# Converting float64 weights on three engines instead of one, in a fused attention and MLP kernel

## The chip, the cores and the metric

The kernel runs on one core of a Trainium2 chip. The metric is the time of one execution on the device in microseconds (us); six executions of the kernel before gave a median of 894.68 us (893.46 to 895.31).

The core has five engines with a queue of instructions each. TensorE (PE in the profile) multiplies matrices and transposes; a matrix multiply in float32 leaves two records in the profile. VectorE (DVE), ScalarE (ACT) and GpSimd (POOL) work on elements. SyncE (SP) only issues data transfers (DMAs) here. An engine works through its queue strictly in order: an instruction that waits for a semaphore holds up all that stands behind it, also where that would have been ready.

## The reference

`x` is 8 batches x 8 heads x 512 positions x 64, `state` is 8 x 8 x 32 x 64, both float32. Attention goes both ways, and its result, 544 rows of 512 for each batch, passes through an MLP:

```
scores  = scale * x @ state.T;     a  = softmax(scores);   xread = a  @ state     # 512 rows of each batch
scores2 = scale * state @ x.T;     a2 = softmax(scores2);  sread = a2 @ x         # 32 rows of each batch
y   = concat([xread, sread]) as (8*544, 512)
h   = y @ w_in                                 # 512 -> 2048
g   = h * erf(softplus(h))
out = g @ w_out                                # 2048 -> 512
```

The weights come as float64: they are made by multiplying a float32 array with a float64 scalar. Each of the two matrices is 8.4 MB. [...] `hi` holds the sign, 11 bits of exponent and the top 20 bits of the fraction, `lo` the other 32 bits.

## The kernel before, in words

**Tiles and stages.** Rows of 128 partitions are used throughout. The hidden width of 2048 is cut into four groups g of 512 (`GF` = 4 blocks of 128 each). The main loop goes over nine chunks: chunk b = 0 to 7 is the 512 x-rows of batch b, chunk 8 is the 256 state rows of all batches. For each chunk and group:

- `mixed(b, g)` (lines 224 to 235) multiplies the batch's states with group g of w_in. As xread is a @ state, the hidden layer of the x-rows is a @ (state @ w_in), which needs a contraction over 256 (8 heads x 32 states) instead of 512. The two halves of the result are copied out of PSUM by ScalarE (line 233) and VectorE (line 234).
- `hidden` (237 to 252) makes h for four blocks: matmuls (246), Softplus on ScalarE (248), a copy of h on VectorE into the tile `hs` (249), then one Erf over all four blocks (250) and one product with `hs` (251). Softplus, Erf and Exp need different tables, and each change of table is an instruction of its own on ScalarE.
- `project` (254 to 260) multiplies the result with group g of w_out (257) and accumulates in PSUM over the groups. It is held back as `pending` and issued after the next group's `hidden`.
- `store` copies the sums out and writes them to memory.

`attention(b)` (139 to 220) transposes x (145), makes the scores (155), copies them to `sc` (159), transposes them back (170), and takes a softmax over the 32 states for the x half (173, 174, 180, 184 to 187); these probabilities are transposed to `aT` (199, 201), an operand of `hidden`. The states' half takes the other softmax, over 512 positions (178, 179, 181), transposes it (193, 195), multiplies with x (212), scales (217), transposes (219) and leaves the result in `sT` (220), which only chunk 8 reads. Attention 0 stands ahead of the main loop; attention b + 1 is issued in group 1 of chunk b.

**Weights.** In chunk 0 each group starts with `weights_in(g)`, `mixed(0, g)` and `weights_out(g)`. Each of the two loads two tiles, so there are 16 weight tiles of 128 x 1024 numbers, 1 MB as float64. `weight` (81 to 110) loads one into the tile `hs`, a pool tag with two buffers that `hidden` uses too, and converts it with seven instructions on VectorE: exponent out of `hi` (96), rebased (98), clamped and put into place (99), sign merged (100), fraction out of `hi` (103), `lo` added (106), fraction times exponent (108).

**Order.** A scheduler places every instruction in its engine's queue when the kernel is built, from the order and dependencies of the program; at run time the queues are fixed. DMAs of SP are in such a queue too. At the start SP issues eight x loads of batch 0 (67), eight state loads (75), two w_in tiles (90), and the x loads of batch 1. A completion semaphore can be shared by several DMAs, and a DMA that uses one again waits for the DMA before.

Of the kernel before, what the change touches and what calls it, by code (L numbers as in the profile page):

```python
# [16 lines left out]
def kernel(  # L17
# [54 lines left out]
    st = const.tile([P, B, P], F32, name="st")  # L72
    for h in range(H):
        i, e = h // 2, h % 2
        nc.sync.dma_start(out=st[Ns * i:Ns * i + Ns, :, D * e:D * e + D],
                          in_=state[:, h].rearrange("b n d -> n b d"))

    w_in = const.tile([P, NK, d_ff], F32, name="w_in")
    w_out = const.tile([P, NF, d_model], F32, name="w_out")

    def weight(dst, src, shape):


        if src.dtype == F32:
            nc.sync.dma_start(out=dst, in_=src)
            return
        i = shape[1]
        n = shape[0] * i
        raw = act.tile([P, 2 * n], U32, name="hs")
        nc.sync.dma_start(out=raw.rearrange("p (o i) -> p o i", i=2 * i), in_=src.bitcast(U32))  # L90
        words = raw.rearrange("p (n w) -> p n w", w=2)
        lo, hi = words[:, :, 0], words[:, :, 1]

        em = act.tile([P, 2, n], U32, name="s", bufs=3)
        e, m = em[:, 0], em[:, 1]
        nc.vector.tensor_scalar(e, hi, 20, 0x7FF, op0=ALU.logical_shift_right,  # L96
                                op1=ALU.bitwise_and)
        nc.vector.tensor_scalar(e, e, -896.0, 0.0, op0=ALU.add, op1=ALU.max)  # L98
        nc.vector.tensor_scalar(e, e, 255.0, 8388608.0, op0=ALU.min, op1=ALU.mult)
        nc.vector.scalar_tensor_tensor(out=e, in0=hi, scalar=0x80000000, in1=e,  # L100
                                       op0=ALU.bitwise_and, op1=ALU.bitwise_or)

        nc.vector.tensor_scalar(m, hi, 0xFFFFF, 0x100000, op0=ALU.bitwise_and,  # L103
                                op1=ALU.bitwise_or)
        f = m.bitcast(F32)
        nc.vector.scalar_tensor_tensor(out=f, in0=lo, scalar=2.0 ** -32, in1=m,  # L106
                                       op0=ALU.mult, op1=ALU.add)
        nc.vector.scalar_tensor_tensor(  # L108
            out=dst, in0=f.rearrange("p (o i) -> p o i", i=i), scalar=2.0 ** -20,
            in1=e.bitcast(F32).rearrange("p (o i) -> p o i", i=i), op0=ALU.mult, op1=ALU.mult)  # L110

    gw = GF * P

    def weights_in(g):
        fs = slice(gw * g, gw * g + gw)
        for k in range(0, NK, 2):
            weight(w_in[:, k:k + 2, fs],
                   moe_w_in[P * k:P * k + 2 * P, fs].rearrange("(k p) f -> p k f", p=P),
                   (2, gw))

    def weights_out(g):
        for t in range(GF * g, GF * g + GF, 2):
            weight(w_out[:, t:t + 2, :],
                   moe_w_out[P * t:P * t + 2 * P].rearrange("(t p) e -> p t e", p=P),
                   (2, d_model))


    sT = const.tile([P, NK, B, Ns], F32, name="sT")
# [8 lines left out]
        nc.scalar.copy(stT[b], ps)  # L137

    def attention(b):
        xt = x_t.pop(b)  # L140
        xT = att.tile([P, NI, S], F32, name="xT")
        for i in range(NI):
            xp = ps_at.tile([P, S], F32, name="at")
            for c in range(NC):
                nc.tensor.transpose(out=xp[:, P * c:P * c + P], in_=xt[:, c, 2 * i:2 * i + 2, :],  # L145
                                    identity=ident)
            nc.scalar.copy(xT[:, i, :], xp)  # L147

        s2 = [ps_at.tile([P, S], F32, name="at") for _ in range(2)]
        for i in range(NI):
            for e in range(2):
                r, q = slice(D * e, D * e + D), slice(Ns * i, Ns * i + Ns)
                nc.tensor.matmul(out=s2[e][q, :], lhsT=stT[b][r, q], rhs=xT[r, i, :],  # L155
                                 start=True, stop=True)
        sc = att.tile([P, 2, S], F32, name="sc")
        for e in range(2):
            nc.scalar.copy(sc[:, e], s2[e])

        a = att.tile([P, 2, NC * NI, Ns], F32, name="a")
        a2 = att.tile([P, 2, S], F32, name="a2")
        a2T = att.tile([P, 2, NC, P], F32, name="a2T")
        aT[b] = keep.tile([P, 2, S], F32, name="aT")
        z2 = small.tile([P, 2], F32, name="z2")
        for e in range(2):

            s1 = ps_at.tile([P, NC * NI, Ns], F32, name="at")
            for c in range(NC):
                nc.tensor.transpose(out=s1[:, NI * c:NI * c + NI, :],  # L170
                                    in_=sc[:, e, P * c:P * c + P], identity=ident)
            m1 = small.tile([P, NC * NI], F32, name="m1")
            nc.vector.reduce_max(out=m1, in_=s1, axis=AX.X)
            nc.vector.tensor_tensor(a[:, e], s1, m1.unsqueeze(2).to_broadcast([P, NC * NI, Ns]),
                                    op=ALU.subtract)

            m2 = small.tile([P, 1], F32, name="m2")
            nc.vector.reduce_max(out=m2, in_=sc[:, e], axis=AX.X)
            nc.vector.tensor_scalar(m2, m2, -scale, None, op0=ALU.mult)
            nc.scalar.activation(out=a[:, e], in_=a[:, e], func=ACTF.Exp, scale=scale)  # L180
            nc.scalar.activation(out=a2[:, e], in_=sc[:, e], func=ACTF.Exp, bias=m2, scale=scale,
                                 accum_out=z2[:, e:e + 1])
            z1 = small.tile([P, NC * NI], F32, name="z1")
            nc.vector.reduce_sum(out=z1, in_=a[:, e], axis=AX.X)
            nc.vector.tensor_scalar(z1, z1, 1e-9, None, op0=ALU.add)
            nc.vector.reciprocal(z1, z1)
            nc.vector.tensor_tensor(a[:, e], a[:, e],
                                    z1.unsqueeze(2).to_broadcast([P, NC * NI, Ns]), op=ALU.mult)

        for e in range(2):  # L190
            ps = ps_at.tile([P, NC, P], F32, name="at")
            for c in range(NC):
                nc.tensor.transpose(out=ps[:, c, :], in_=a2[:, e, P * c:P * c + P],  # L193
                                    identity=ident)
            nc.scalar.copy(a2T[:, e], ps)
        for e in range(2):
            ps = ps_at.tile([P, S], F32, name="at")
            for c in range(NC):
                nc.tensor.transpose(out=ps[:, P * c:P * c + P],  # L199
                                    in_=a[:, e, NI * c:NI * c + NI, :], identity=ident)  # L200
            nc.vector.tensor_copy(aT[b][:, e], ps)

        nc.vector.tensor_scalar(z2, z2, 1e-9, None, op0=ALU.add)
        nc.vector.reciprocal(z2, z2)
        sr = ps_at.tile([P, 2, D], F32, name="at")
        for e in range(2):
            for c in range(NC):
                for i in range(NI):  # L210
                    q = slice(Ns * i, Ns * i + Ns)
                    nc.tensor.matmul(out=sr[q, e, :], lhsT=a2T[:, e, c, q],  # L212
                                     rhs=xt[:, c, 2 * i + e, :],
                                     start=(c == 0), stop=(c == NC - 1))
        sn = small.tile([P, 2, D], F32, name="sn")
        for e in range(2):
            nc.vector.tensor_scalar(sn[:, e], sr[:, e], z2[:, e:e + 1], None, op0=ALU.mult)
        ps = ps_at.tile([P, NI, Ns], F32, name="at")
        nc.tensor.transpose(out=ps, in_=sn, identity=ident)
        nc.scalar.copy(sT[:, :, b, :], ps)  # L220

    m_t = {}

# [62 lines left out]
                for k in range(NK)]  # L286

    states(0)
    attention(0)
    chunks = [(S, put_x(b)) for b in range(B)] + [(B * Ns, put_s)]  # L290
    pending = None
    for b, (n, put) in enumerate(chunks):
        acc = None
        for g in range(NG):
            if b == 0:
                weights_in(g)
                mixed(0, g)
                weights_out(g)
            if b + 1 < B and g == 0:
                load_x(b + 1)  # L300
                states(b + 1)
            gT = hidden(pairs(b, g), n)
            if pending is not None:
                pending()
            if acc is None:
                acc = [ps_o.tile([P, d_model], F32, name="o%d" % r) for r in range(n // P)]

            def pending(gT=gT, n=n, g=g, acc=acc, put=put):
                project(gT, n, g, acc)
                if g == NG - 1:  # L310
                    store(acc, n, put)
            if b + 1 < B:
                mixed(b + 1, g)
                if g == 1:
                    attention(b + 1)
    pending()


# [28 lines left out]
```

## Time and profile before

| what | value |
|---|---|
| median of six executions | 894.68 us |
| the profiled execution | 893.46 us, of it 891.7 us between the first and the last instruction (span) |
| mean granted TensorE clock | 0.976 of full speed |
| busy time of TensorE | 836.6 us (94%) |
| busy time of VectorE | 355.2 us (40%) |
| busy time of ScalarE | 351.8 us (39%) |
| busy time of GpSimd | 0.7 us |
| median from issue to landing, 1 MB w_in tile | 5.2 us |
| median from issue to landing, 128 KB x load | 3.0 us |

The shares of busy time are means over two very different stretches, the loading and converting of weights at the start and the rest, and so have to be read by windows. A line of a table of groups names the source line, the engine, the operation, the written and read tiles, the shape and the count; then the busy time in us and the mean of one in ns, then the idle time in front of them and what ended it. A line of the chain of waits has a start, a length and what took it: the chain is followed back from the last instruction to what released it.

### The profile page before, as it was taken

Reading aid. Unit: us, or ns where it says so; the run is one execution under the profiler, and the core shown is the slowest. Engines: PE = TensorE matmul, PEld = TensorE weight load, DVE = VectorE, ACT = ScalarE, POOL = GpSimd, SP = SyncE. Lnnn points to the kernel's source line nnn. Section 1 sums busy time; section 2 is a strip of 40 time slices with the busy share of each in tenths; the row PEclk is TensorE's granted clock in tenths of the full one; section 3 lists DMA queues with packets and bytes.
Section 4 is the critical chain, followed back from the end, with each engine's and each line's share of the span. In section 5 each row is a group of like instructions: output and inputs, shape, how many; then the busy total and the mean of one; then the engine's idle time right before and its main releaser. Section 6 shows DMA issues by size and latency. Waiting matters only on the chain.

```text
span 891.7 us, 7809 instructions
## 1 busy us (share of the span) xinstructions
PE 836.6 (94%) x3216; PEld 379.2 (43%) x3216; DVE 355.2 (40%) x500; ACT 351.8 (39%) x460; POOL 0.7 (0%) x6
## 2 busy tenths in 40 slices
PE   3659868999999999999999999999999999999997
PEld 1313423344444444445444544444444444445664
DVE  3888988523422252226222522234222522222121
ACT  2221530544434453437333633444344534333342
POOL 0000000000000000000000000000000000000000
PEclk9579988999999999999999999999999999999999
DMA  8432254010201020101000020100010000000100
GB/s 212 142 133 103 95 142 142 0 48 0 49 0 48 0 49 0 39 10 36 13 24 24 1 48 0 48 0 1 0 48 0 1 1 35 12 0 1 47 1 24
DMA packets 45346, 35.09 MB, mean 39 GB/s; under 512 B 36864, under 2 KB 36864, under 8 KB 45312
## 3 DMA queue, kind: packets, MB, share of 16 engines
q1 hardware_dynamic: 45312, 34.61, 12.7%
q8 instruction: 25, 0.41, 0.2%
q14 instruction: 9, 0.07, 0.0%
HBM read 25.69 MB, written 8.91 MB: 39 GB/s over the span
## 4 chain that ended last, share of the span: by engine, by line
PE 83%; DVE 11%; DMA 3%; SPq 1%; ACT 1%; issue 0%; DVEq 0%
PE o L257 49%; PE h L246 26%; PE at L231 3%; DMA hs<-in_moe_w_in_dram 2%; DVE s L106 2%; DVE s L100 2%; PE at L145 1%; DVE s L251 1%; DVE s L96 1%; PE at L212 1%; DVE s L103 1%; DVE s L98 1%; DMA hs<-in_moe_w_out_dram 1%; PE at L155 1%; PE at L199 1%; PE at L193 1%
## 5 line engine op out<-in xcount | busy, mean ns | idle before, releaser
L257 PE MATMUL o<-w_out,s 128*128 128x512 f32 x1088 | 488.6, 597 | 14.9 <-DVE s L251 14.9
L257 PEld LDWEIGHTS o<-w_out,s 128*128 128x128 f32 x1088 | 204.1, 191 | 260.4 <-issue 241.1
L246 PE MATMUL h<-aT,m 128*128 128x512 f32 x512 | 242.2, 609 | 6.5 <-DVE hs L249 6.5
L249 DVE COPY hs<-h 128x512 f32<-128x512 f32 (+1 forms) x144 | 95.1, 661 | 247.1 <-ACT s L248 247.1
L248 ACT ACTIVATE s<-h 128x512 f32<-128x512 f32 (+1 forms) x144 | 82.3, 574 | 186.9 <-PE h L246 186.5
L246 PEld LDWEIGHTS h<-aT,m 128*128 128x128 f32 x512 | 94.5, 193 | 132.1 <-issue 117.8
L251 DVE TENSOR_TENSOR s<-s,hs 128x2048 f32<-128x2048 f32 (+1 forms) x36 | 78.2, 2173 | 74.7 <-ACT s L250 74.7
L233 ACT COPY m<-at 128x512 f32<-128x512 f32 x32 | 18.7, 586 | 210.8 <-PE at L231 210.8
L234 DVE COPY m<-at 128x512 f32<-128x512 f32 x32 | 22.1, 691 | 166.4 <-PE at L231 166.4
L250 ACT ACTIVATE s<-s 128x2048 f32<-128x2048 f32 (+1 forms) x36 | 65.3, 1815 | 0.4
L248 ACT ACT_TABLE_LOAD x42 | 53.9, 1283 | 14.2 <-DVE w_out L108 13.5
L231 PE MATMUL at<-w_in,stT 64*32 64x512 f32 x512 | 42.4, 622 | 6.0 <-DVE w_in L108 5.6
L250 ACT ACT_TABLE_LOAD x36 | 46.2, 1283 | 0.6
L265 ACT COPY ot<-o 128x512 f32<-128x512 f32 x34 | 19.8, 582 | 65.1 <-PE o L257 65.1
L246 PE MATMUL h<-sT,w_in 128*128 128x256 f32 x128 | 28.9, 379 | 0.0
L246 PEld LDWEIGHTS h<-sT,w_in 128*128 128x128 f32 x128 | 24.3, 190 | 6.7 <-issue 3.8
L231 PEld LDWEIGHTS at<-w_in,stT 64*32 64x32 f32 x512 | 6.7, 106 | 35.4 <-issue 22.6
L145 PE MATMUL at<-ident,x 128*128 128x128 f32 x128 | 18.4, 293 | 2.3 <-DVE m L234 2.1
L145 PEld LDWEIGHTS at<-ident,x 128*128 128x128 f32 x128 | 16.1, 151 | 10.2 <-ACT m L233 3.0
L96 DVE TENSOR_SCALAR s<-hs 128x1024 uint32<-128x1024 uint32 x16 | 11.0, 690 | 23.4 <-DMA hs<-in_moe_w_in_dram 22.4
L147 ACT COPY xT<-at 128x512 f32<-128x512 f32 x32 | 17.4, 590 | 7.1 <-PE at L145 7.1
L106 DVE SCALAR_TENSOR_TENSOR s<-hs,s 128x1024 f32<-128x1024 uint32 x16 | 19.5, 1221 | 0.1
(47 smaller groups left out, 296.2 us busy)
## 6 DMA issues: line engine op xcount, KB each, us to landing
x<-in_x_dram SPq DMA_DIRECT2D x64, 128.0 KB, 3.0
hs<-in_moe_w_in_dram SPq DMA_DIRECT2D x8, 1024.0 KB, 5.2
hs<-in_moe_w_out_dram SPq DMA_DIRECT2D x8, 1024.0 KB, 5.5
out_dram<-ot SPq DMA_DIRECT2D x32, 256.0 KB, 2.3
st<-in_state_dram SPq DMA_DIRECT2D x8, 64.0 KB, 2.1
out_dram<-ot SPq DMA_DIRECT2D x8, 64.0 KB, 1.7
```

The costliest lines, as they stand in the source:

```text
L96: nc.vector.tensor_scalar(e, hi, 20, 0x7FF, op0=ALU.logical_shift_right, op1=ALU.bitwise_and)
L106: nc.vector.scalar_tensor_tensor(out=f, in0=lo, scalar=2.0 ** -32, in1=m, op0=ALU.mult, op1=ALU.add)
L145: nc.tensor.transpose(out=xp[:, P * c:P * c + P], in_=xt[:, c, 2 * i:2 * i + 2, :], identity=ident)
L231: nc.tensor.matmul(out=ps[e][q, :], lhsT=stT[b][r, q], rhs=w_in[r, i, gw * g:gw * g + gw], start=True, stop=True)
L234: nc.vector.tensor_copy(mg[:, 1], ps[1])
L246: nc.tensor.matmul(out=hp[:, 0:n], lhsT=lhsT[:, P * i:P * i + P], rhs=rhs, start=(k == 0), stop=(k == len(pairs) - 1))
L248: nc.scalar.activation(out=s[:, i, :], in_=hp[:, 0:n], func=ACTF.Softplus)
L249: nc.vector.tensor_copy(hs[:, i, :], hp[:, 0:n])
L250: nc.scalar.activation(out=s, in_=s, func=ACTF.Erf)
L251: nc.vector.tensor_tensor(s, s, hs, op=ALU.mult)
L257: nc.tensor.matmul(out=acc[r], lhsT=gT[:, i, P * r:P * r + P], rhs=w_out[:, GF * g + i, :], start=(g == 0 and i == 0), stop=(g == NG - 1 a ...
L265: nc.scalar.copy(ot, acc[r])
```

## The change

Four things change.

1. The conversion. `hi`, read as a float32 number, has the float64's exponent in the wrong place by three bits. It is multiplied by 2^-112 (GpSimd), which rebases the exponent; the bits are shifted left by 3 (VectorE), which makes room for the lower bits and drops the old sign; `lo` is scaled by 2^-29 into an integer of up to 3 bits (ScalarE); both are added as integers (GpSimd); and the sign bit of `hi` is merged in (VectorE). The steps work in place in the destination, the scaling in place in the raw tile.
2. The raw tiles of w_in have a tag `raw` with two buffers of their own; those of w_out stay with `hs`. The tag `s` isn't used by the conversion any more.
3. The eight state loads are issued from ScalarE's queue.
4. The states' half of `attention` becomes an inner function `rest`. For batch 0 it is called after `hidden` of chunk 0, group 0; for the others right after `attention`.

```
-        nc.sync.dma_start(out=st[Ns * i:Ns * i + Ns, :, D * e:D * e + D],
-                          in_=state[:, h].rearrange("b n d -> n b d"))
+        nc.scalar.dma_start(out=st[Ns * i:Ns * i + Ns, :, D * e:D * e + D],
+                            in_=state[:, h].rearrange("b n d -> n b d"))
...
-    def weight(dst, src, shape):
+    def weight(dst, src, shape, tag, bufs):
...
-        n = shape[0] * i
-        raw = act.tile([P, 2 * n], U32, name="hs")
-        nc.sync.dma_start(out=raw.rearrange("p (o i) -> p o i", i=2 * i), in_=src.bitcast(U32))
-        words = raw.rearrange("p (n w) -> p n w", w=2)
-        lo, hi = words[:, :, 0], words[:, :, 1]
-
-        em = act.tile([P, 2, n], U32, name="s", bufs=3)
-        e, m = em[:, 0], em[:, 1]
-        nc.vector.tensor_scalar(e, hi, 20, 0x7FF, op0=ALU.logical_shift_right,
-                                op1=ALU.bitwise_and)
-        nc.vector.tensor_scalar(e, e, -896.0, 0.0, op0=ALU.add, op1=ALU.max)
-        nc.vector.tensor_scalar(e, e, 255.0, 8388608.0, op0=ALU.min, op1=ALU.mult)
-        nc.vector.scalar_tensor_tensor(out=e, in0=hi, scalar=0x80000000, in1=e,
+        raw = act.tile([P, 2 * shape[0] * i], U32, name=tag, bufs=bufs)
+        raw = raw.rearrange("p (o i) -> p o i", i=2 * i)
+        nc.sync.dma_start(out=raw, in_=src.bitcast(U32))
+        words = raw.rearrange("p o (i w) -> p o i w", w=2)
+        lo, hi = words[:, :, :, 0], words[:, :, :, 1]
+        d = dst.bitcast(U32)
+        nc.gpsimd.tensor_scalar(dst, hi.bitcast(F32), 2.0 ** -112, None, op0=ALU.mult)
+        nc.scalar.activation(out=lo, in_=lo, func=ACTF.Copy, scale=2.0 ** -29)
+        nc.vector.tensor_scalar(d, d, 3, None, op0=ALU.logical_shift_left)
+        nc.gpsimd.tensor_tensor(d, d, lo, op=ALU.add)
+        nc.vector.scalar_tensor_tensor(out=d, in0=hi, scalar=0x80000000, in1=d,
                                        op0=ALU.bitwise_and, op1=ALU.bitwise_or)
-
-        nc.vector.tensor_scalar(m, hi, 0xFFFFF, 0x100000, op0=ALU.bitwise_and,
-                                op1=ALU.bitwise_or)
-        f = m.bitcast(F32)
-        nc.vector.scalar_tensor_tensor(out=f, in0=lo, scalar=2.0 ** -32, in1=m,
-                                       op0=ALU.mult, op1=ALU.add)
-        nc.vector.scalar_tensor_tensor(
-            out=dst, in0=f.rearrange("p (o i) -> p o i", i=i), scalar=2.0 ** -20,
-            in1=e.bitcast(F32).rearrange("p (o i) -> p o i", i=i), op0=ALU.mult, op1=ALU.mult)
...
-                   (2, gw))
+                   (2, gw), "raw", 2)
...
-                   (2, d_model))
+                   (2, d_model), "hs", 2)
...
+        def rest():
+            a2 = att.tile([P, 2, S], F32, name="a2")
...
+        return rest
...
-    attention(0)
+    rest = attention(0)
...
             gT = hidden(pairs(b, g), n)
+            if b == 0 and g == 0:
+                rest()
             if pending is not None:
                 pending()
...
-                    attention(b + 1)
+                    attention(b + 1)()
```

The queues of the changed kernel, as its build fixes them, differ from those of before at these places. On VectorE the first reduction of attention 0 stands behind the shift of w_out's second tile; the copy of mixed(0,0) behind the merge of the third w_in tile; the product of chunk 0, group 0 behind the shift of the third w_out tile. On ScalarE the copy of the first states behind the scaling of the first w_in tile, and the copies of the scores behind the scaling of the second w_out tile. On TensorE hidden(0,1) stands behind the first matmul of group 0's projection, where before it stood ahead of all of it. On SP all four weight loads of group 0 stand ahead of the x loads of batch 1, and the last two w_out loads behind the x loads of batch 3.

## The prediction

> **What bounds the kernel now.** I read the page's totals first, then busy time by stretches of 20 us, then the groups of the first 165 us, then the chain and the order of time there. The stretches split the run in two (per stretch: length, busy PE, PEld, DVE, ACT, POOL, then the granted clock, the DMA share and GB/s):
>
> ```profile
> 20.00:40.00 20.00, 10.48 (x98) 5.01 (x97) 17.74 (x34) 4.52 (x10) 0.00 (x0) 0.58 0.56 151
> 60.00:80.00 20.00, 16.07 (x43) 5.70 (x44) 17.22 (x20) 0.94 (x2) 0.00 (x0) 0.83 0.44 158
> 120.00:140.00 20.00, 10.16 (x32) 3.33 (x27) 16.08 (x19) 6.81 (x8) 0.00 (x0) 0.74 0.30 96
> ...
> 0.00:165.00 165.00, 115.82 (x532) 48.44 (x532) 131.27 (x181) 45.70 (x67) 0.70 (x6) 0.88 0.43 131
> 165.00:891.70 726.70, 720.77 (x2690) 330.79 (x2684) 223.88 (x319) 306.12 (x393) 0.00 (x0) 1.00 0.06 19
> ```
>
> From 165 us on TensorE is busy without gaps at full clock, and the change touches nothing there. Before it VectorE (DVE) is the full engine, and TensorE has holes in which its clock drops to a half. The conversions fill VectorE (busy us, mean ns of one):
>
> ```profile
> L106 DVE SCALAR_TENSOR_TENSOR s<-hs,s 128x1024 f32<-128x1024 uint32 x16 | 19.5, 1221 | 0.1
> L100 DVE SCALAR_TENSOR_TENSOR s<-hs,s 128x1024 uint32<-128x1024 uint32 x16 | 19.5, 1220 | 0.0
> L98 DVE TENSOR_SCALAR s<-s 128x1024 uint32<-128x1024 uint32 x16 | 11.0, 686 | 0.0
> ```
>
> Back to back they start 0.60 us (one input) and 1.13 us (two inputs) apart, as the chain of waits shows, with the product that ends group 0 and the rate of TensorE once it runs (start, us, what):
>
> ```profile
> 58.08 1.13 DVE s L106
> 59.22 1.13 DVE s L100
> 60.35 2.21 DVE s L251
> ...
> 70.10 0.69 DVE s L96
> ...
> 123.57 0.61 DVE hs L249
> ...
> 154.33 5.15 PE o L257 x12
> ```
>
> So the measure for the change is TensorE's lost time: time passed less its work at full clock, 0.43 us per 512-wide record (5.15/12). By 165 us TensorE did 96 projection and 64 hidden records (160 x 0.43 = 68.8), 8 mixed (1.1 each, 8.8) and two attentions (7.4 each, 14.8): 92.4, so 72.6 us are lost. Only that can shrink.
>
> **Part by part.** *VectorE.* A tile's seven instructions (4 x 0.60 + 3 x 1.13 = 5.8 us, 93 over 16 tiles) become a shift and a sign merge (0.60 + 1.13, 28 in all): 65 us off the full engine.
>
> *ScalarE* gets 16 scalings of 128x1024. Between 0.62 us (Exp, 512 wide) and 1.91 us (Erf, 2048 wide) a straight line gives 1.05: 17 us on an engine that is busy 45.7 of 165. The price is their place in the queue, below.
>
> *GpSimd (POOL)* gets 16 multiplies M and 16 integer adds A, and has no such row. The nearest:
>
> ```profile
> 1.00 0.29 POOL masks.py:199 TENSOR_SCALAR_AFFINE_SELECT ident<-ident 128x128 f32<-128x128 f32 x1
> ...
> masks.py:197 POOL MEMSET ident<- 128x128 f32 x1 | 0.2, 204 | 0.3 <-POOLq L331 0.3
> L331 POOL MEMSET const-float32-0.0<- 128x1 f32 x1 | 0.1, 98 | 0.2 <-issue 0.2
> ```
>
> The select's growth, (0.292 - 0.098)/127 = 1.5 ns an element, gives M = 1.6 at 1024. Bounds: the memset's growth, 0.8 ns, gives 0.9; eight selects give 2.3. A reads two inputs: at least VectorE's 1.13, at most two of the long M, 4.7; I take 1.5 M = 2.4. M + A is then 4.0 per tile, bounds 2.1 to 7.0.
>
> *Loads.* The eight state loads (0.45 us of issue each, 6.1 to 10.2 us on SP) go to ScalarE's queue, behind nothing. The first weight load can issue at about 6.2 instead of 10.25, the other three of group 0 right after (w_out no longer waits for a buffer). x and states (1.57 MB at the 200 GB/s of 4 to 8 us) end near 9; a 1 MB weight tile takes 2.6 us at the 400 GB/s seen at 14 to 16 us. Estimated landings: 12, 14.6, 17.2, 19.8. The first transpose could start at 9.3 instead of 12.5, but its copy on ScalarE is queued behind the scaling of w_in's first tile (12 + 1.05), so that gain is not used. The second batch's x loads on SP now stand behind all of group 0's weights; needed first near 87 us, free. The third batch's wait for the postponed states' half, but stand behind a w_out load that waits longer: free.
>
> *Walk with M = 1.6, A = 2.4.* The order of each queue is fixed by the build.
> 1. VectorE's first attention instruction is queued behind the shift of w_out's second tile, whose release runs through GpSimd: from 14.6, three M, three A and two shifts: 14.6 + 12 + 1.2 = 27.8 (before 19.6). ScalarE's score copies wait behind the fourth scaling (20.9): no later than that. The attention then needs 9 us instead of 11 (states' half gone): aT ready at 36.8 (before 30.7).
> 2. Before, mixed(0,0) waited for w_in's conversion until 37.7 and its copy ended at 40.4. Now w_in is ready at 19.7, but mixed follows aT on TensorE (38.6) and its VectorE copy is queued behind the merge of the next w_in tile (shift 37.4, A 39.8, merge 40.9): 41.5. One us lost.
> 3. Group 0's Erf ends at 56.3, but its product (line 251) is queued behind the shift of w_out(1), and GpSimd works there without pause from 50.4 (two A, two M, shifts and merges between): the product ends at 61.8, before 62.56. TensorE has by then not done hidden(0,1), which before stood ahead; it starts at 64.9 with 18.5 us of work done (attention 7.4, hidden 6.9, three mixed 3.3, one projection 0.9). Lost: 46.4.
> 4. From there TensorE mostly runs. Stalls left: 2.5 for the half clock at the start; 1.8 at 90 (x transposes behind the scaling of w_out(2), whose load waits for product(0,1)); about 2 in attention 1; 5.0 near 125 (hidden(0,2)'s last softplus behind the scaling of w_out(3), whose load stands on SP behind eight x loads that wait for attention 1's last read of x); 4.7 near 133 (a hidden copy behind the last shift). Sum 16.
>
> Lost 46.4 + 16 = 62.4 against 72.6: 10.2 us gained. Hand-overs take some back: the chain's "issue" pieces are 0.02 to 0.14; four a tile at 0.07 on the seven tiles of the path: 2. *Sum: -8 us.* On the profiled execution (span 891.7, time 893.46) that is a span of 883.5 and 885.3; against the median of the six, 894.68, 1.2 above the profiled run, 886.7.
>
> *Postponed states' half:* two reductions, two Exp, 8 transposes, 64 small matmul records, two copies. It leaves step 1 and fills TensorE's wait in hidden(0,0); the cover is that wait for softplus and hidden copies (before: 45.7 to 49.9). Without it, it costs about 3 us of TensorE.
>
> *A rule against the change.* Row: one-input VectorE instructions go 1024 elements in 0.60 us, two-input ones in 1.13, so the former run at double rate. The Trainium skill, SBUF — State Buffer, section "Who interferes with whom", says that a double-rate VectorE instruction, or one with two SBUF inputs beside a GpSimd read, shares a port pair with GpSimd as an exclusive lock: the second to start waits for the whole of the first. By rows alone no lock is in the sum; by the rule each shift and merge may wait up to an A, and with one wait of half an A on each of seven tiles the 8 us are gone. No row here shows both engines at work.
>
> **Rivals.**
> - *GpSimd sets the pace (slower).* Per us of M + A the path grows by some 7: three tiles in step 1, half in 2, two in 3, about 1.5 in 4. Slower from M + A = 4.0 + 8/7, or 5.1. At the bound 7.0: +21, 908. For: three steps of the walk already end on GpSimd, two inputs may cost double. Against: the select row is a small tile with its fixed cost in it.
> - *Collisions or hand-overs eat the gain (no change to slightly slower)*: 894 to 899, seven tiles at 1.2 us or a bit more. For: VectorE's products and merges overlap GpSimd's work. Against: VectorE is now free over half of the time.
> - *GpSimd cheap (much faster).* M + A = 2.1 gives -1.9 x 7 = -13 more: 873. Then step 1 ends on ScalarE's score copies (22.7), and steps 2 to 4 on loads. For: the memset's growth. Against: A reads two streams.
> - *The moved loads do nothing*: part of the forecast; if the copy did not wait, at most 3 us more.
>
> **How the numbers follow.** Forecast 0.50 (878 to 892); GpSimd pace 0.20; collisions 0.12; cheap GpSimd 0.18. The prediction is the likeliest case's 887. The range takes in most of the cheap and of the pace case: 870 to 904. Half of the collisions count as slower, the rest is split between no change and faster (0.02): faster by over 0.2% (1.8 us, about what a measurement of this kernel can tell from no change) 0.70, within 0.04, slower 0.26.
>
> **What would show it.** In the profile after: VectorE's conversion groups at 28 us instead of 93; GpSimd's multiplies near 1.6 and adds near 2.4; VectorE's first reduction near 28 waiting for a GpSimd result; hidden(0,0) near 40; the product of group 0 near 62; TensorE without gaps from about 140 instead of 171. I am wrong if GpSimd's spacing is over 5 us a tile, if its durations swell where VectorE works, or if step 1's VectorE wait ends on something else. The later 730 us should not change.

## The result, and the profile after

The changed kernel takes 899.06 us (median of 21 runs) against 894.53 for the kernel before (47 runs): a ratio of 1.0049, 95% interval 1.0038 to 1.0060. It is slower by half a per cent, where 887 was forecast. The profiled execution has a span of 896.7 us, 5.0 more than before.

The busy time by stretches, of the profile after (columns as in the prediction):

```profile
0.00:165.00 165.00, 107.62 (x508) 45.53 (x509) 81.23 (x103) 66.55 (x86) 88.79 (x38) 0.84 0.43 131
165.00:896.70 731.70, 726.81 (x2709) 335.22 (x2707) 223.66 (x318) 304.01 (x390) 0.00 (x0) 1.00 0.06 18
```

VectorE was relieved as intended: 81.2 us busy by 165 us instead of 131.3. TensorE still did less in that time than before (508 records instead of 532), at a mean clock of 0.84 instead of 0.88. The rest of the run is as it was. So the 5 us lie in the start, and the 50 us taken off VectorE brought TensorE nothing. GpSimd has come in with 88.8 us. The groups of the first 165 us, of after (busy us, mean ns of one | idle time before, and who ended it):

```profile
L96 POOL TENSOR_SCALAR w_in<-raw 128x1024 f32<-128x1024 f32 x8 | 23.1, 2885 | 14.6 <-DMA raw<-in_moe_w_in_dram 14.6
L96 POOL TENSOR_SCALAR w_out<-hs 128x1024 f32<-128x1024 f32 x8 | 22.6, 2831 | 37.5 <-DMA hs<-in_moe_w_out_dram 37.5
L99 POOL TENSOR_TENSOR w_out<-w_out,hs 128x1024 uint32<-128x1024 uint32 x8 | 21.9, 2739 | 6.1 <-DVE w_out L98 6.1
L99 POOL TENSOR_TENSOR w_in<-w_in,raw 128x1024 uint32<-128x1024 uint32 x8 | 20.8, 2604 | 10.1 <-DVE z L197 5.2 <-DVE w_in L98 3.3 <-ACT raw L97 0.9
L100 DVE SCALAR_TENSOR_TENSOR w_in<-raw,w_in 128x1024 uint32<-128x1024 uint32 x8 | 15.0, 1881 | 13.9 <-POOL w_in L99 13.9
L100 DVE SCALAR_TENSOR_TENSOR w_out<-hs,w_out 128x1024 uint32<-128x1024 uint32 x8 | 11.2, 1401 | 12.0 <-POOL w_out L99 12.0
L98 DVE TENSOR_SCALAR w_in<-w_in 128x1024 uint32<-128x1024 uint32 x8 | 9.3, 1167 | 22.0 <-POOL w_in L96 21.9
L98 DVE TENSOR_SCALAR w_out<-w_out 128x1024 uint32<-128x1024 uint32 x8 | 6.4, 804 | 10.3 <-POOL w_out L96 10.3
```

Two things are to be seen. The multiply takes 2.8 to 2.9 us, more than the add with its two inputs (means 2.60 and 2.74 us, medians 2.40 and 2.39). And the shift and the sign merge have swollen: 1.17 and 1.88 us on w_in's tiles, where the same kinds of instruction took 0.69 and 1.22 us before. VectorE waits 58 us for GpSimd (21.9 + 13.9 + 12.0 + 10.3). The order of time on GpSimd, of after, shows the start (start, length, and in brackets the idle time before):

```profile
14.29 2.85 POOL L96 TENSOR_SCALAR w_in<-raw 128x1024 f32<-128x1024 f32 x1 [13.01 <-DMA raw<-in_moe_w_in_dram]
17.32 3.27 POOL L96 TENSOR_SCALAR w_in<-raw 128x1024 f32<-128x1024 f32 x1 [0.17 <-DMA raw<-in_moe_w_in_dram]
20.55 2.41 POOL L99 TENSOR_TENSOR w_in<-w_in,raw 128x1024 uint32<-128x1024 uint32 x1
23.66 3.23 POOL L99 TENSOR_TENSOR w_in<-w_in,raw 128x1024 uint32<-128x1024 uint32 x1 [0.70 <-ACT hs L97]
26.87 2.80 POOL L96 TENSOR_SCALAR w_out<-hs 128x1024 f32<-128x1024 f32 x1
...
32.88 2.81 POOL L96 TENSOR_SCALAR w_out<-hs 128x1024 f32<-128x1024 f32 x1
```

and the same stretch on VectorE, of after:

```profile
20.62 2.90 DVE L98 TENSOR_SCALAR w_in<-w_in 128x1024 uint32<-128x1024 uint32 x1 [2.74 <-POOL w_in L96]
...
35.73 0.69 DVE L98 TENSOR_SCALAR w_out<-w_out 128x1024 uint32<-128x1024 uint32 x1 [0.68 <-POOL w_out L96]
36.34 0.68 DVE L184 TENSOR_REDUCE m<-sc 128x1 f32<-128x512 f32 x1
```

GpSimd hardly pauses from 14.3 to 35.7, and the first reduction of attention 0 starts at 36.34, behind the shift of w_out's second tile, as the walk said it would, but 8.5 us later than the walk had it. TensorE waits for what follows from it, in one piece of 17.4 us:

```profile
43.54 1.94 PE L175 MATMUL at<-ident,a 128*128 128x128 f32 x8 [17.42 <-DVE a L169]
```

The second w_in tile's multiply begins at 17.32, 0.17 us after the first has ended, and what it waited for was its load. The shift that starts at 20.62, while GpSimd adds, takes 2.90 us instead of 0.69; it ends 0.56 us after the add.

One more reading, from the chain of waits of after:

```profile
7.61 9.87 DMA st<-in_state_dram
17.48 0.20 issue
17.68 0.46 PE at L126
```

The state loads are issued early on their own queue, but the last lands 9.9 us after its issue (median of the eight 3.4, before 2.1), among the weight tiles: the DMA engines are busy at a share of 1.0 from 4 to 20 us. TensorE's first transpose starts at 17.7 us instead of 12.5.

### The profile page after: what moved, and what is told of

It is laid out like the page before. It is cut to its first block, busy times and chain, and to the rows that moved or that the text cites. A ratio compares the mean times of both kernels' runs of the same rounds, so it can differ in the third digit from the quotient of the medians.

```text
span 896.7 us, 7819 instructions
## 1 busy us (share of the span) xinstructions
PE 834.4 (93%) x3216; PEld 380.8 (42%) x3216; DVE 304.9 (34%) x420; ACT 370.6 (41%) x476; POOL 88.8 (10%) x38
## 3 DMA queue, kind: packets, MB, share of 16 engines
q1 hardware_dynamic: 43136, 34.09, 12.3%
## 4 chain that ended last, share of the span: by engine, by line
PE 87%; POOL 5%; DVE 3%; DMA 3%; ACT 1%; issue 1%; SPq 0%; ACTq 0%; POOLq 0%; DVEq 0%
PE o L251 51%; PE h L240 28%; PE at L225 3%; POOL w_in L99 2%; POOL w_out L96 2%; PE at L137 1%; DMA st<-in_state_dram 1%; DMA hs<-in_moe_w_out_dram 1%; PE at L147 1%; PE at L175 1%; PE at L204 1%; POOL w_out L99 1%; PE at L192 1%; PE at L158 1%; POOL w_in L96 1%
## 5 line engine op out<-in xcount | busy, mean ns | idle before, releaser
L240 PE MATMUL h<-aT,m 128*128 128x512 f32 x512 | 245.0, 615 | 6.4 <-DVE hs L243 4.2
L228 DVE COPY m<-at 128x512 f32<-128x512 f32 x32 | 22.1, 690 | 178.0 <-PE at L225 177.9
L96 POOL TENSOR_SCALAR w_out<-hs 128x1024 f32<-128x1024 f32 x8 | 22.6, 2831 | 37.5 <-DMA hs<-in_moe_w_out_dram 37.5
L175 PE MATMUL at<-ident,a 128*128 128x128 f32 x64 | 9.4, 292 | 17.5 <-DVE a L169 17.4
L96 POOL TENSOR_SCALAR w_in<-raw 128x1024 f32<-128x1024 f32 x8 | 23.1, 2885 | 14.6 <-DMA raw<-in_moe_w_in_dram 14.6
L99 POOL TENSOR_TENSOR w_out<-w_out,hs 128x1024 uint32<-128x1024 uint32 x8 | 21.9, 2739 | 6.1 <-DVE w_out L98 6.1
L99 POOL TENSOR_TENSOR w_in<-w_in,raw 128x1024 uint32<-128x1024 uint32 x8 | 20.8, 2604 | 10.1 <-DVE z L197 5.2
```

The lines of the kernel that those rows point to most:

```text
L96: nc.gpsimd.tensor_scalar(dst, hi.bitcast(F32), 2.0 ** -112, None, op0=ALU.mult)
L99: nc.gpsimd.tensor_tensor(d, d, lo, op=ALU.add)
L228: nc.vector.tensor_copy(mg[:, 1], ps[1])
L240: nc.tensor.matmul(out=hp[:, 0:n], lhsT=lhsT[:, P * i:P * i + P], rhs=rhs, start=(k == 0), stop=(k == len(pairs) - 1))
```

## The experiments

Theory 1: GpSimd's part of a tile is longer than I had it, and its queue sets the pace. Theory 2: the late state loads hold everything up. Theory 3, from the port rule in the prediction: GpSimd and VectorE hold each other up, whether or not one waits for the other's result. A ratio is to the kernel before.

### The old conversion, all else kept

```
-        nc.gpsimd.tensor_scalar(dst, ...), nc.scalar.activation(...), ...   # the five instructions
+        e, m = em[:, 0], em[:, 1]                                           # the seven of before
```

> The changed kernel with the conversion of before (seven VectorE instructions), all else kept: w_in's own raw buffers, state loads on ScalarE's queue, postponed states' half. Theory 1 (GpSimd's queue sets the pace, M = 2.8 and A = 2.4 us): without GpSimd the other parts show their own worth, about 3 us from the postponed half and a few from the buffers: 886 to 892, faster than before. Theory 2 (the late state loads, first transpose at 17.7 instead of 12.5, hold everything up): it stays at 897 to 900, VectorE's first reduction late too.

879.5 us, ratio 0.983 (0.980 to 0.986). That is faster than theory 1 had it (886 to 892). The other parts of the change gain 15.5 us, and the new conversion takes 19.6 us (899.1 - 879.5), more than all of it. The first transpose is as late as in after (18.05), so theory 2 falls as the cause.

### State loads back on SP

```
-        nc.scalar.dma_start(out=st[...
+        nc.sync.dma_start(out=st[...
```

> The changed kernel with the eight state loads on SP ahead of the weights, as before; all else as after. Theory 1: the first transpose is back at about 12.5 but the attention still waits for GpSimd: 896 to 899, at most 2 us under after. Theory 2: about 5 us under after, 894.

898.2 us, ratio 1.0041 (1.0025 to 1.0056), the same as after within the intervals. The first transpose is back at 12.3, and nothing came of it: TensorE then waits 16.1 us in one piece for attention 0's probabilities.

### The states' half back in its place

```
-    rest = attention(0)
+    attention(0)()
...
-            if b == 0 and g == 0:
-                rest()
```

> The changed kernel with the states' half of attention 0 back in its place. Both theories: two VectorE reductions, two Exp and the transposes return to the way to aT, 2 to 4 us over after: 901 to 903. If the postponing is what costs, it is faster than after.

903.9 us, ratio 1.0104 (1.0077 to 1.0131): 5 us over after. Beside the new conversion the postponing is worth its place.

### The multiply on ScalarE

```
-        nc.gpsimd.tensor_scalar(dst, hi.bitcast(F32), 2.0 ** -112, None, op0=ALU.mult)
+        nc.scalar.activation(out=dst, in_=hi.bitcast(F32), func=ACTF.Copy, scale=2.0 ** -112)
```

> The changed kernel with the multiply by 2^-112 on ScalarE instead of GpSimd, which keeps the integer add. Theory 1: GpSimd's share of a tile falls from 5.2 to 2.4 us, at 7 tiles on the path 20 us less, part of it given back by 16 more scalings on ScalarE: 878 to 885. Theory 2: no change, 897 to 900. If ScalarE's queue is what holds up (scalings wait for loads ahead of copies), slower than after.

877.5 us, ratio 0.981 (0.979 to 0.984): 21.5 us under after. GpSimd's busy time falls to 40.8 us. In this build the shift of w_out's second tile also stands behind the first reductions of attention 0, so a part of the 21.5 may be order.

### The multiply on VectorE

```
-        nc.gpsimd.tensor_scalar(dst, hi.bitcast(F32), 2.0 ** -112, None, op0=ALU.mult)
+        nc.vector.tensor_scalar(dst, hi.bitcast(F32), 2.0 ** -112, None, op0=ALU.mult)
```

> The changed kernel with the multiply on VectorE (0.60 us a tile), GpSimd keeps the integer add. Theory 1 (GpSimd's pace): as with the multiply on ScalarE, M + A falls from 5.2 to 2.4, some 20 us under after: 875 to 880. Theory 3 (port lock: VectorE's fast instructions and GpSimd hold each other up): three lock-prone VectorE instructions a tile instead of two beside the add, so it stays several us above the ScalarE variant's 877.5: 880 to 888.

885.4 us, ratio 0.991 (0.989 to 0.993), 8 us above the ScalarE variant, as theory 3 expected. This doesn't single out theory 3, as VectorE's queue also has 16 instructions more here. VectorE's shifts of w_in take 1208 ns and w_out's multiplies 962, where one alone takes 0.69 us.

### No GpSimd

```
-        nc.gpsimd.tensor_scalar(dst, hi.bitcast(F32), 2.0 ** -112, None, op0=ALU.mult)
-        nc.scalar.activation(out=lo, in_=lo, func=ACTF.Copy, scale=2.0 ** -29)
-        nc.vector.tensor_scalar(d, d, 3, None, op0=ALU.logical_shift_left)
-        nc.gpsimd.tensor_tensor(d, d, lo, op=ALU.add)
+        nc.vector.tensor_scalar(dst, hi.bitcast(F32), 2.0 ** -112, None, op0=ALU.mult)
+        nc.scalar.activation(out=lo, in_=lo, func=ACTF.Copy, scale=2.0 ** -29, bias=-0.499)
+        nc.vector.scalar_tensor_tensor(out=d, in0=d, scalar=3, in1=lo,
+                                       op0=ALU.logical_shift_left, op1=ALU.bitwise_or)
```

> No GpSimd in the conversion: multiply on VectorE, shift and merge of the low bits in one VectorE instruction (a bitwise or instead of the add; ScalarE's scaling has a bias of -0.499, so that the low bits are cut off rather than rounded and can't carry), sign merge as after. VectorE 0.60 + 1.13 + 1.13 = 2.9 us a tile, 46 in all instead of 93. Theory 1: one queue and two hand-overs less a tile: 868 to 877. Theory 3: no lock either, the same. If VectorE's busy time set the pace rather than GpSimd, worse than the add-only variants: 880 or more.

869.3 us, ratio 0.972 (0.968 to 0.975): 30 us under after, with more work on VectorE (50 us of conversion).

### The same, with GpSimd work that nobody waits for

```
+    nc.gpsimd.memset(w_out[:, 12:16, :], 1.0)
+    for _ in range(14):       # v: w_out[:, 12:16] as pairs of words, y: w_out[:, 10:12]
+        nc.gpsimd.tensor_scalar(y, v[:, :, :, 1], 1.0, None, op0=ALU.mult)
+        nc.gpsimd.tensor_tensor(y.bitcast(U32), y.bitcast(U32), v.bitcast(U32)[:, :, :, 0], op=ALU.add)
```

> The variant without GpSimd, with 14 multiplies and 14 integer adds of the same shapes and strides on GpSimd that nobody waits for (they write a part of w_out that is overwritten later), from the start to about 75 us. Queues of all other engines are the same. Theory 1: no wait, so within 2 us of the variant without them. Theory 3: VectorE's conversion groups grow from 0.69 and 1.22 us towards 1.2 and 1.9 as in after, and the time by 3 to 10 us.

890.6 us, ratio 0.995 (0.994 to 0.997): 21 us over the variant without GpSimd, where theory 3 had 3 to 10. VectorE never waits for a GpSimd result here; its instructions only take longer. The groups of VectorE in the first 165 us, without GpSimd:

```profile
L98 DVE SCALAR_TENSOR_TENSOR w_in<-w_in,raw 128x1024 uint32<-128x1024 uint32 x8 | 9.8, 1224 | 1.1 <-ACT raw L97 1.0
L99 DVE SCALAR_TENSOR_TENSOR w_in<-raw,w_in 128x1024 uint32<-128x1024 uint32 x8 | 9.7, 1218 | 0.0
L96 DVE TENSOR_SCALAR w_in<-raw 128x1024 f32<-128x1024 f32 x8 | 5.5, 687 | 18.6 <-DMA raw<-in_moe_w_in_dram 18.6
```

and with that work beside them:

```profile
L98 DVE SCALAR_TENSOR_TENSOR w_in<-w_in,raw 128x1024 uint32<-128x1024 uint32 x8 | 15.7, 1969 | 0.2
L99 DVE SCALAR_TENSOR_TENSOR w_in<-raw,w_in 128x1024 uint32<-128x1024 uint32 x8 | 14.5, 1821 | 0.0
L96 DVE TENSOR_SCALAR w_in<-raw 128x1024 f32<-128x1024 f32 x8 | 13.1, 1641 | 15.5 <-DMA raw<-in_moe_w_in_dram 15.5
...
L166 DVE TENSOR_REDUCE m<-at 128x16 f32<-128x512 f32 x4 | 2.6, 679 | 0.0
L167 DVE TENSOR_TENSOR a<-at,m 128x512 f32<-128x512 f32 x4 | 2.6, 678 | 0.0
```

One-input instructions (the ones that the prediction calls double-rate, here the fast mode) grow from 0.69 to 1.64 us and those with two SBUF inputs from 1.22 to 1.8 to 2.0. Reductions, and a subtraction whose large input comes from PSUM, keep their 0.68. Not every group with two SBUF inputs grew: w_out's merges stayed at 1.22 and the 2048-wide product (L250) at 2.29, where an add on GpSimd beside it took 3.71 us and so was the one that waited; w_out's multiplies went to 1.06 only. VectorE's conversion takes 76.5 us in all instead of 50.0. This is theory 3 by itself, and it contradicts what I expected of theory 1.

### Memsets that nobody waits for

```
-    for _ in range(14): ... tensor_scalar, tensor_tensor
+    for _ in range(40):
+        nc.gpsimd.memset(w_out[:, 12:16, :], 1.0)
```

> The variant without GpSimd, with 40 memsets of 128x2048 on GpSimd (1.8 us each, to about 75 us) that nobody waits for, in place of multiplies and adds. If GpSimd's reads hold VectorE up, no change from the variant without them (869); if its writes do too, the fast one-input VectorE instructions grow and the time rises by 3 to 15 us; two-input ones stay at 1.22.

871.3 us, ratio 0.974 (0.971 to 0.976), 2 us over the variant without, which is within the intervals. VectorE's groups, with the memsets:

```profile
L96 DVE TENSOR_SCALAR w_in<-raw 128x1024 f32<-128x1024 f32 x8 | 10.2, 1275 | 16.8 <-DMA raw<-in_moe_w_in_dram 16.8
L98 DVE SCALAR_TENSOR_TENSOR w_in<-w_in,raw 128x1024 uint32<-128x1024 uint32 x8 | 9.7, 1218 | 1.0 <-ACT raw L97 0.8
L99 DVE SCALAR_TENSOR_TENSOR w_in<-raw,w_in 128x1024 uint32<-128x1024 uint32 x8 | 9.7, 1217 | 0.0
```

GpSimd instructions that only write hold up the fast one-input instructions (0.69 to 1.28) and leave those with two inputs alone. Together the two runs agree with the Trainium skill, SBUF — State Buffer, section "Who interferes with whom": the fast mode takes the whole shared port pair, a second SBUF input only its reading side. That the second to start waits for the whole of the first, as the prediction's rule has it, fits the shift of 2.90 us above, but by the recorded spans not every pair: in the run with multiplies and adds, a VectorE multiply at 76.73 us took 1.60 us beside a GpSimd multiply that ran from 75.81 to 79.51. Which of the two waits, and how long, was not worked out further.

### The multiply twice

```
         nc.gpsimd.tensor_scalar(dst, hi.bitcast(F32), 2.0 ** -112, None, op0=ALU.mult)
+        nc.gpsimd.tensor_scalar(dst, dst, 1.0, None, op0=ALU.mult)
```

> The changed kernel with each GpSimd multiply done twice (the second by 1.0). Theory 1: 2.8 us more a tile at 7 tiles on the path, 15 to 22 us over after: 912 to 921. Theory 2 (late state loads): no change.

921.8 us, ratio 1.031 (1.029 to 1.034): 22.8 us over after for 2.9 us more a tile, 7.9 per us. The walk had some 7.

### Half of the multiply on VectorE

```
-        nc.gpsimd.tensor_scalar(dst, hi.bitcast(F32), ...)
+        nc.gpsimd.tensor_scalar(dst[:, 0:1, :], hi.bitcast(F32)[:, 0:1, :], ...)
+        nc.vector.tensor_scalar(dst[:, 1:2, :], hi.bitcast(F32)[:, 1:2, :], ...)
```

> The changed kernel with half of each multiply (512 elements) on VectorE, so that GpSimd's multiply takes about 1.5 us, the size the prediction gave it, and M + A 3.9. If the mis-sized multiply was the whole error, 1.35 us less a tile at 7 to 8 a us: 885 to 889, as predicted. If the port lock takes its own share, 890 to 896: the three VectorE instructions before and after the add still collide with GpSimd.

892.0 us, ratio 0.997 (0.996 to 0.999). The second multiply, in the order of time:

```profile
16.90 1.77 POOL L96 TENSOR_SCALAR w_in<-raw 128x512 f32<-128x512 f32 x1 [1.57 <-DMA raw<-in_moe_w_in_dram]
```

GpSimd's multiply takes 1.5 to 1.7 us here (medians 1520 and 1657 ns): the size that the prediction gave it. That is worth 7 us; 5 us to the forecast of 886.7 remain. They are not all collisions: the half on VectorE adds 9.1 us to its queue, and the second w_in tile again lands near 17 instead of 14.6: the first multiply is done 1.57 us before.

### Sizes of GpSimd instructions

```
+    nc.gpsimd.tensor_scalar(y, v[:, :, :, 1], 1.0, None, op0=ALU.mult)         # step of two words
+    nc.gpsimd.tensor_scalar(z, y, 1.0, None, op0=ALU.mult)                     # step one
+    nc.gpsimd.tensor_scalar(z[:, 0, 0:256], y[:, 0, 0:256], 1.0, None, op0=ALU.mult)
+    nc.gpsimd.tensor_tensor(z.bitcast(U32), y.bitcast(U32), y.bitcast(U32), op=ALU.add)
```

> The variant without GpSimd, with four GpSimd instructions that nobody waits for, before any VectorE work: the multiply of 1024 with the step of two words that the raw tile has, the same with step one, with step one of 256, and the integer add of 1024 with step one. If the step makes the multiply dear, the second takes about 1.6 us, else 2.8; if the cost is by element, the third takes 0.7. The time stays within 2 us of 869.3.

In the order of time, beside the select that the prediction had used as its row:

```profile
2.69 0.29 POOL masks.py:199 TENSOR_SCALAR_AFFINE_SELECT ident<-ident 128x128 f32<-128x128 f32 x1
2.96 2.81 POOL L106 TENSOR_SCALAR w_out<-w_out 128x1024 f32<-128x1024 f32 x1
5.85 2.77 POOL L107 TENSOR_SCALAR w_out<-w_out 128x1024 f32<-128x1024 f32 x1
8.70 0.85 POOL L108 TENSOR_SCALAR w_out<-w_out 128x256 f32<-128x256 f32 x1
9.63 1.89 POOL L109 TENSOR_TENSOR w_out<-w_out 128x1024 uint32<-128x1024 uint32 x1
```

The step isn't what makes the multiply dear (2.81 against 2.77); it costs (2.77 - 0.85)/768 = 2.5 ns an element, the select 1.5. The spacing of the starts says the same as the lengths: 2.89, 2.85 and 0.93 us. One run gave 864.1 us, 5 below the variant without GpSimd, outside the 2 that I expected; with a single run this stays open.

### What the other parts are worth

The next three runs put parts together without the new conversion. First w_in's own raw buffers alone, in the kernel before:

```
-        raw = act.tile([P, 2 * n], U32, name="hs")
+        raw = act.tile([P, 2 * n], U32, name=tag, bufs=bufs)      # "raw", 2 for w_in; "hs", 2 for w_out
```

> The kernel before with one change: w_in's raw tiles have two buffers of their own. If the shared buffers bounded the kernel before (weight loads wait for VectorE, VectorE for weight loads), most of the 18 us that the same with the state loads on ScalarE's queue gained: 876 to 884. If VectorE's conversion time bounded it, 890 to 895.

877.9 us, ratio 0.981 (0.979 to 0.983): 17 us by this part alone, with all seven VectorE instructions in place. VectorE's waits in its first 165 us:

```profile
DVE s L98 <- DMA raw<-in_moe_w_in_dram: 15.8, 1, 15.8
DVE hs L254 <- ACT s L253: 7.0, 5, 2.7
```

against those of the kernel before:

```profile
DVE s L96 <- DMA hs<-in_moe_w_in_dram: 22.4, 5, 15.5
DVE hs L249 <- ACT s L248: 6.0, 4, 2.2
```

Before, VectorE ran dry of w_in's loads five times, 6.9 us beside the first; now only the first load makes it wait. w_in's last tile is issued at 94.7 us instead of 136.2, as its load no longer waits for hidden's product to give the shared buffer back. The 6.9 us are less than the 17 gained. TensorE's waits for VectorE's group products and for converted w_in in the same 165 us, before:

```profile
PE o L257 <- DVE s L251: 13.9, 2, 7.3
...
PE at L231 <- DVE w_in L108: 5.6, 3, 2.4
```

and with the buffers:

```profile
PE at L236 <- DVE w_in L110: 12.2, 3, 5.5
...
PE o L262 <- DVE s L256: 0.7, 2, 0.5
```

TensorE has done 560 records by then instead of 532, at a mean clock of 0.92 instead of 0.88. How the 17 us divide between these was not separated.

Then the buffers and the state loads' queue, and the buffers and the postponed half:

```
# the old conversion with own raw buffers, and
+    attention(0)()                      # first run: states' half in place, state loads on ScalarE's queue
+        nc.sync.dma_start(out=st[...    # second run: states' half postponed, state loads on SP
```

> The conversion of before with w_in's own buffers and the state loads on ScalarE's queue, the states' half back ahead of the main loop. The changed kernel lost 5 to 7 us by that; here too: 884 to 888. What then is left under before (894.2) is the worth of the buffers.

> The conversion of before with w_in's own buffers and the postponed states' half, but the state loads on SP ahead of the weights: it leaves the buffers and the half. If the state loads' new queue is worth something, slower than 879.5 (the same with ScalarE's queue); if it costs, as the first transpose at 18.1 instead of 12.5 suggests, 874 to 878.

876.7 us, ratio 0.979 (0.975 to 0.983), and 883.5 us, ratio 0.986 (0.981 to 0.991). The first is far under the 884 to 888 expected. With the two earlier runs all four places have a time: states' half in place, loads on SP 877.9 and on ScalarE's queue 876.7; half postponed, loads on SP 883.5 and on ScalarE's queue 879.5. So beside the old conversion the buffers alone give what all other parts together give. The postponed half looks like a loss of 3 to 6 us, and the loads' queue like a gain of 1 to 4, but the intervals of the ratios overlap or touch.

And the changed kernel with shared buffers again:

```
-                   (2, gw), "raw", 2)
+                   (2, gw), "hs", 2)
```

> The changed kernel with w_in's raw tiles back among the shared buffers. If the buffers are worth as much here as beside the old conversion, 10 to 18 us over after: 909 to 917. If GpSimd's queue and the port hide it, within 3 us of after: 897 to 902.

902.0 us, ratio 1.0082 (1.0060 to 1.0104), 3 us over after, where the intervals just touch. Of the 17 us that the buffers are worth alone, at most some 3 are left beside the new conversion.

### Without GpSimd: order and place

Three variants of the kernel without GpSimd: state loads on SP, the states' half in its place, the multiply on ScalarE.

```
+        nc.sync.dma_start(out=st[...                                             # first
+    attention(0)()                                                               # second
+        nc.scalar.activation(out=dst, in_=hi.bitcast(F32), func=ACTF.Copy, ...)  # third
```

> The variant without GpSimd, with the state loads on SP ahead of the weights. The first transpose at 12.5 instead of 17.8, and in the build the first attention stands ahead of w_out's conversion on VectorE: 862 to 868 against 869.3. If the attention is held by the weights anyway, the same 869.

> The variant without GpSimd, with the states' half of attention 0 back ahead of the main loop. With the conversion of before the early half was 3 us better than the late one; with VectorE as free as here the late half has less to hide behind: 863 to 872 against 869.3. The changed kernel had lost 5 us by it; if that was its own worth, 874.

> The variant without GpSimd, with the multiply on ScalarE too: VectorE 2.3 us a tile, ScalarE 2.3. If VectorE still sets the pace at the start, 864 to 868; if ScalarE's queue does (its scalings stand ahead of copies that TensorE waits for), 870 to 875.

865.4 us, ratio 0.967 (0.962 to 0.971); 871.6, ratio 0.973 (0.970 to 0.976); 871.9, ratio 0.974 (0.972 to 0.977). The first is the fastest of the variants that were timed more than once: 3.3% under before. Against the variant without GpSimd (869.3, ratio 0.968 to 0.975) the state loads' own queue seems to cost 4 us, where it seemed to give 1 to 4 beside the old conversion, and the late half to gain 2; all three intervals overlap with that one, so none of these is a price. Moving the multiply from VectorE to ScalarE gains nothing, which suggests, but doesn't show, that VectorE is no longer the limit.

## Why the prediction was wrong

**What bounds the kernel.** The prediction said "before it VectorE (DVE) is the full engine". It was nearly full, but its work was not the only bound: with the same VectorE work and two more buffers the kernel is 17 us faster. With about half of the conversion's work on VectorE as well (50 us without GpSimd, 102 before, all else as in the changed kernel) it gains another 10 (869.3 against 879.5). Of the 23 us of VectorE's idle time that ended with a load, 15.5 were the first load, which the buffers don't shorten; the rest, and TensorE's 13.9 us of waits for group products, stood in the profile. The sum used w_in's own buffers only in the landings of group 0 and left this gain out. It doesn't show in the total, because the new conversion takes 19.6 us where all other parts together give 15.5.

**The multiply, M = 1.6.** This term failed. It measured 2.8, outside the bounds that the prediction gave for it (0.9 to 2.3). The growth of another instruction, the select, was taken for the multiply's. A = 2.4 was right (2.40). M + A came to 5.2, and the rival "GpSimd sets the pace" was to decide from 5.1: its point, its mechanism and, with 7.9 us per us measured against 7, its slope held. At 7 a us, M + A = 5.2 by itself gives 895 (886.7 + 8.4); the rest of the way to 899.1 isn't explained by the multiply's size. Giving the multiply nearly its predicted size gave 7 us back, and left 5.

**"By rows alone no lock is in the sum".** The second failed step. The lock was in the prediction as a rule and a rival, and the sum had it at nothing. In the kernel without GpSimd, idle GpSimd work alone costs 21 us. In the changed kernel VectorE's shifts and merges take 42 us (15.0 + 11.2 + 9.3 + 6.4) instead of the 30.6 of 16 x (0.69 + 1.22), 11 us more. How the remaining 5 us to the forecast divide between collisions, later loads and hand-overs was not separated.

**The walk, step by step.** Step 1: 36.3 against 27.8. The second multiply began at 17.3 and not at 14.6, because its tile landed later than estimated (2.7 us; with a shorter first multiply it still waited for the load until 16.9); three multiplies, 3.3, 2.8 and 2.8, were 4.1 longer than 1.6 each; one add waited 0.7 for a scaling and took 0.8 more. That is 8.3 of 8.5. Step 2 (mixed(0,0) copied at 52.1 instead of 41.5) and step 3 (product of group 0 at 75.6 instead of 61.8) followed from the same queue. Step 4 was near: 13.8 us late at the product, 13.2 late at the end (span 896.7 against 883.5). So the placing of the waits was right, and their sizes were not. Two slips of the walk changed nothing: by its own terms w_in is ready at 22.1 (14.6 + 1.6 + 4.8 + 1.1) and not at 19.7, and 885.3 and 1.2 make 886.5, not 886.7.

**The loads.** "The first transpose could start at 9.3" was wrong: it started at 17.7, as the state loads were on the way beside 1 MB weight tiles. That by itself cost nothing in the changed kernel, as GpSimd was later (898.2 with the loads on SP). The estimated landing of w_in's second tile, 14.6, was wrong too, and its 2.7 us are part of step 1.

**The postponed half.** "Without it, it costs about 3 us": 5 measured in the changed kernel. Without GpSimd it seemed to gain 2, and beside the old conversion to lose 3 to 6, neither clear of the intervals.

## What to carry to other kernels

A full engine need not be the only bound: see first what ends its idle time, and whether a buffer that two loops share lets its loads come too late. Work moved to GpSimd has to be priced with that very instruction, and with what it does to VectorE: fast one-input instructions and those with two SBUF inputs can be held up while GpSimd reads (here to 1.6 and 1.8 to 2.0 us, from 0.69 and 1.22), whether or not one waits for the other's result. The step that is cheapest to try, one more buffer tag, gained 17 us, while the clever conversion on three engines lost 19.6.

## What was not expected of the hardware

- GpSimd's multiply by a constant in float32 costs 2.5 ns an element (2.77 us for 128x1024), dearer than its integer add of two inputs (1.89 with step one, 2.37 to 2.39 with one input at a step of two words).
- A one-input VectorE instruction on a 128x2 tile took 1.76 us with idle GpSimd work beside it (0.16 without): here the hold-up did not depend on how much VectorE had to do. The add that ran on GpSimd meanwhile ended at 50.05.

```profile
48.31 1.76 DVE L202 TENSOR_SCALAR z<-z 128x2 f32<-128x2 f32 x1
```

- A load's landing depended on what stood in other queues: eight 64 KB state loads on ScalarE's queue took up to 9.9 us from issue to landing, where on SP ahead of the weights they took 2.0 to 2.7.
